# Raw score products of the first pair moved up, in place of products of zeros

## The chip, the cores and the metric

The kernel runs on one core of one Trainium2 chip. The metric is the device time of one execution in microseconds, and lower is better. The time before is the median of three runs.

## The reference

The program is attention, followed by two feed-forward layers. Queries, keys and values come as 2 x 12 heads of 448 positions and 64 elements, all in float32. Cut to what matters here:

```
scores = scale * q @ k.T               # each head: 448 x 448, k=64
scores = where(mask, -1e9, scores)     # causal: later positions masked
scores = scores - max(scores, axis=-1)
attn   = exp(scores); attn = attn / (sum(attn) + 1e-9)
x      = attn @ v                      # 896 tokens x 768
h      = x @ w_in                      # 768 -> 1024, then h * softmax(h), layer norm, g_ln
y      = ln @ w_out                    # 1024 -> 768
out    = max(y @ w_in2, 0)**2 @ w_out2 # 768 -> 2048 -> 768
```

## The kernel before

**Pairs.** Attention works on twelve pairs of heads (pair 0 to pair 11), two heads side by side in the upper and lower 64 partitions. A pair goes through these steps, each with a short name and the pair's number behind a point:

- `load_r`: SP issues the transfer of keys and queries into a buffer `KQ` (four of them).
- `H`: ScalarE copies them, rounded for faster products, to `HI` (three of them).
- `S0c`, `S0a`, `S0b`: TensorE multiplies the rounded copies into a PSUM tile `mxp`, only to find each row's maximum (L253). Each of the three takes a PSUM bank.
- `mxc`, `mxa`, `mxb`: VectorE adds the mask and reduces each product to its maxima `mx` (L268); a reduction is one instruction, and a second one reads its accumulator. Then the bank is given back.
- `mT`, `row`, `rowd`: TensorE transposes the maxima (L280), ScalarE copies them, and SP sends them through DMA into a row `MR` (L297, L298). For pair 0 alone this is replaced by `mxr`: ScalarE copies the maxima to `mr` (L292) and they are subtracted by products with a negative identity (L330).
- `Sa`, `Sb`: the scores of the first and the second half, transposed, into a PSUM tile `s`: first the raw products of keys and queries in full float32 (L311, four products per half, shown as eight records), then the products that subtract the maxima (L330 for pair 0: ten per half; L322 for the others).
- `ea1`, `eb1`: ScalarE takes the exponential of a half into `PP` and gives the bank back (L346).
- `ka`, `kb`, `ad`: GpSimd zeroes the masked half and adds rows. `Ua`, `Ub`, `Us`: TensorE multiplies by the values and sums. Then follow the division, transfers and further steps.

**Order.** The order of all steps on all engines is written out by hand, in one list of names `SEQ`. Each engine takes its own steps out of it, in the list's order, and waits by semaphore for what the other engines must have done. The transfers all go through SP's queue, in the list's order as well.

**Banks.** During attention there are four double banks of PSUM. `bank2` takes the first of a list of free ones when the program is built, and `give` puts a bank back at the list's end. The order of takes and gives in `SEQ` thus sets which bank a step uses and which earlier step it waits for.

**Products of zeros.** `fill(n)` takes a bank, issues `n` products of a tile of zeros (L528) and gives the bank back. The step `fl` calls `fill(2)` whatever its number, and `f1` calls `fill(1)`. Their results are never read.

The start of `SEQ` before:

```
fl.0 load_r.0 H.0 fl.1 fl.2 fl.3 fl.4 f1.0 S0c.0 S0a.0 S0b.0 fl.5 fl.6 fl.7 mxc.0 load_r.1 mxa.0 fl.8 mxb.0 lq.0 H.1 mxr.0
S0b.1 S0a.1 load_r.2 Sa.0 mxb.1 S0c.1 mxa.1 H.2 load_r.3 mxc.1 S0a.2 ea1.0 S0b.2 mT.1 Sb.0 row.1 H.3 ld.3 load_v.0
```

After attention come the two feed-forward layers, whose products (L499 `h`, L656 `y`, L913 `ab`, L1124 `o`) take up the rest of the time. Weights of the first are loaded during attention (`lq`, `ld`).

Of the kernel before, what the change touches and what calls it, by code (L numbers as in the profile page):

```python
# [25 lines left out]
ATT = ("recips", "rcd", "spread", "norm", "x_hi", "x_lo", "E", "Ua", "Ub", "sums")  # L26

SEQ = """
fl.0 load_r.0 H.0 fl.1 fl.2 fl.3 fl.4 f1.0 S0c.0 S0a.0 S0b.0 fl.5 fl.6 fl.7 mxc.0 load_r.1 mxa.0 fl.8 mxb.0 lq.0 H.1 mxr.0
S0b.1 S0a.1 load_r.2 Sa.0 mxb.1 S0c.1 mxa.1 H.2 load_r.3 mxc.1 S0a.2 ea1.0 S0b.2 mT.1 Sb.0 row.1 H.3 ld.3 load_v.0  # L30
mxb.2 lq.1 rowd.1 mxa.2 S0c.2 ka.0 S0b.3 Sa.1 load_r.4 load_v.1 eb1.0 kb.0 mxc.2 ad.0 mT.2 mxb.3 ea1.1 ka.1 lq.2 Sb.1
row.2 S0a.3 S0c.3 Ua.0 load_v.2 rowd.2 H.4 Ub.0 load_r.5 mxa.3 eb1.1 mxc.3 lq.3 S0c.4 kb.1 S0a.4 ad.1 mT.3 Us.0 row.3
Sa.2 mxa.4 E.0 S0b.4 sums.0 ea1.2 Sb.2 mxc.4 mxb.4 recips.0 eb1.2 Ua.1 H.5 Ub.1 load_v.3 lq.8 mT.4 rowd.3 wf.0 Us.1
S0b.5 rcd.0 row.4 Sa.3 load_r.6 E.1 ea1.3 H.6 S0a.5 lq.4 ka.2 mxb.5 Sb.3 mxa.5 eb1.3 S0c.5 rowd.4 Sa.4 ea1.4 mxc.5
Sb.4 kb.2 ad.2 mT.5 S0a.6 ka.3 S0b.6 sums.1 kb.3 spread.0 recips.1 row.5 mxa.6 eb1.4 norm.0 Ua.2 load_r.7 x_hi.0 rcd.1
Ub.2 Us.2 ka.4 S0c.6 H.7 load_v.4 lq.5 mxb.6 rowd.5 E.2 spread.1 mxc.6 Ua.3 S0a.7 x_lo.0 mT.6 sums.2 Ub.3 ad.3 row.6
lq.6 load_r.8 mxa.7 kb.4 S0c.7 rowd.6 S0b.7 recips.2 Us.3 Sb.5 rcd.2 lq.7 norm.1 wh.0 mxc.7 E.3 mxb.7 sums.3 x_hi.1
Ua.4 eb1.5 ad.4 H.8 Sa.5 lq.9 ea1.5 mT.7 x_lo.1 row.7 Sb.6 spread.2 S0b.8 eb1.6 kb.5 Sa.6 S0a.8 recips.3 ea1.6
load_r.9 Ub.4 wf.1 mxb.8 Us.4 S0c.8 mxa.8 H.9 norm.2 E.4 rowd.7 ka.5 mxc.8 rcd.3 Sa.7 S0a.9 load_v.5 Sb.7 ea1.7 mT.8
ad.5 S0b.9 mxa.9 S0c.9 load_r.10 x_hi.2 row.8 Ua.5 kb.6 spread.3 x_lo.2 mxb.9 ka.6 norm.3 Ub.5 sums.4 load_v.6 ad.6  # L40
load_g.0 rowd.8 Us.5 ka.7 wh.1 mxc.9 recips.4 wl.1 Sa.8 H.10 eb1.7 S0a.10 E.5 mT.9 kb.7 load_v.7 Sb.8 ea1.8 S0b.10
rcd.4 load_r.11 row.9 S0c.10 sums.5 mxa.10 mxb.10 Ua.6 Ub.6 mxc.10 spread.4 eb1.8 x_hi.3 Us.6 H.11 x_lo.3 kb.8 lq.10
rowd.9 load_v.8 recips.5 mT.10 norm.4 S0b.11 row.10 rcd.5 mxb.11 E.6 ad.7 ka.8 S0a.11 mxa.11 Ua.7 Ub.7 Sa.9 ad.8
S0c.11 rowd.10 mxc.11 Sb.9 ld.4 mT.11 ea1.9 Sa.10 row.11 eb1.9 wl.0 x_hi.4 Sb.10 sums.6 x_lo.4 rowd.11 Us.7 lq.11
load_v.9 ea1.10 spread.5 Ua.8 eb1.10 Ub.8 kb.9 norm.5 Sb.11 Sa.11 recips.6 Us.8 wf.2 eb1.11 lw.0 wf.3 ea1.11 wh.2 E.7
h1.0 x_hi.5 ld.5 wl.2 wh.3 h1.1 wl.3 rcd.6 ka.9 spread.6 ka.10 x_lo.5 wf.4 kb.11 norm.6 h0.0 ka.11 wh.4 h0.1 h2.0 h1.2
kb.10 sums.7 recips.7 wf.5 rcd.7 E.8 load_v.10 h2.1 sums.8 h2.2 lw.1 h1.3 wl.4 ad.9 h0.2 h2.3 Ua.9 wh.5 x_hi.6 Ub.9
h0.3 wl.5 x_lo.6 recips.8 h0.4 spread.7 h0.5 h1.4 lw.2 h1.5 mx.0 mx.1 ex.0 Us.9 norm.7 E.9 rcd.8 mu.0 h2.4 h2.5 Ua.10
ex.1 sq.0 load_v.11 sums.9 Ub.10 Ua.11 x_hi.7 Ub.11 ad.10 de.0 mu.1 va.0 ad.11 spread.8 recips.9 de.1 Us.10 x_lo.7
sq.1 norm.8 va.1 E.10 mx.2 of.0 rcd.9 sums.10 ex.2 x_hi.8 recips.10 Us.11 x_lo.8 spread.9 pw.0 fa.0 h4.0 h5.0 mu.2  # L50
norm.9 rcd.10 h4.1 h5.1 E.11 pw.1 h5.2 of.1 h4.2 h3.0 sums.11 spread.10 recips.11 ln.0 x_hi.9 x_lo.9 fa.1 h3.1 sq.2
rcd.11 de.2 T.0 h3.3 oh.0 norm.10 x_hi.10 va.2 h3.2 h5.3 ol.0 ln.1 x_lo.10 pw.2 spread.11 Th.0 lw.3 oh.1 of.2 Tl.0
norm.11 ol.1 h3.4 x_hi.11 h4.4 T.1 x_lo.11 of.3 h3.5 mx.3 fa.2 oh.2 h5.4 Th.1 Tl.1 h4.3 h4.5 oh.3 ex.3 ln.2 mu.3 de.3
mx.4 h5.5 sq.3 ex.4 mx.5 va.3 T.2 lw.4 h6.0 ex.5 pw.3 h6.2 lw.5 mu.4 h6.4 de.4 h6.3 de.5 fa.3 lw.6 sq.4 ln.3 T.3 Th.2
mu.5 h6.1 lw.7 Th.3 ol.2 sq.5 Tl.2 Tl.3 va.4 pw.4 h6.5 va.5 mx.6 ol.3 ex.6 fa.4 y0.0 mu.6 of.4 sq.6 of.5 pw.5 oh.4
y0.1 de.6 ol.4 fa.5 of.6 y0.2 oh.5 ln.4 va.6 ln.5 ol.5 oh.6 y0.3 pw.6 y0.4 ol.6 T.4 y0.5 fa.6 Th.4 Tl.4 of.7 ln.6 T.5
y0.6 Th.5 Tl.5 T.6 oh.7 Th.6 ol.7 r2.0 r2.1 y0.7 Tl.6 y1.0 yo.0 yo.1 yo.2 qr.0 r2.2 qh.0 qg.0 qr.1 r2.3 qh.2 qg.2 qr.5
r2.5 s1.1 qr.4 r2.4 s2.1 s4.1 y1.1 yp.0 xt.0 xt.1 yd.0 y1.2 yp.1 xt.2 xl.0 yd.1
"""


def attention_moe_kernel(tc, kq, v, w_in, w_out, g_ln, w_in2, w_out2, out):
# [7 lines left out]
    NP, P, _, S = kq.shape  # L70
    D = P // 2
    DM, NT = out.shape
    H = DM // D
# [19 lines left out]
    with es:  # L93
# [71 lines left out]
        def bank2(nm):  # L165

            pl = slots.pop(0)
            t = pl.tile([P, 2, 512], F32, tag="b", name=nm)
            slot_of[id(t)] = (pl, t)
            return t  # L170
# [9 lines left out]
        with att:  # L180
# [52 lines left out]
            mx = {}  # L233
            mr = {}
            UB = {}
            sb = {}
# [40 lines left out]
            def max_T(i):  # L277

                b = st.pop(("c", i))
                nc.tensor.transpose(b[0:8, 0, 512 - JP :], mx.pop(i), ident[:JP, :JP])  # L280
                return b

            def max_row(i, T):
                st["m2", i] = m2 = work.tile([8, JP], F32R, tag="m2", name="m2")
                nc.scalar.copy(m2, T[0:8, 0, 512 - JP :])
                give(T)
# [14 lines left out]

            HALF = (((0, 64, 0, 448), (3, 0, 384, 64)), ((1, 192, 128, 320), (2, 0, 256, 192)))

            def scores(n):
                i, a = divmod(n, 2)
                K, Q = (KQ[i % NKQ][:, j] for j in range(2))
                s = sb[n] = bank2("s")
                for t, o, q0, nq in HALF[a]:
                    for h in range(2):
                        r = slice(D * h, D * h + D)  # L310
                        nc.tensor.matmul(  # L311
                            s[:, h, o : o + nq],
                            K[r, P * t : P * t + P],
                            Q[r, q0 : q0 + nq],
                            start=t == HALF[a][0][0],
                            stop=False,
                        )

                for o, x, n in () if i in mr else (((0, 0, D + S),), ((192, D + P, S - P), (0, D + 2 * P, S - 2 * P)))[a]:
                    for h in range(2):  # L320
                        r = slice(D * h, D * h + D)
                        nc.tensor.matmul(  # L322
                            s[:, h, o : o + n], NEG1[r], MR[i % 3][r, x : x + n], start=False, stop=o == 0
                        )
                for t, o, q0, nq in HALF[a] if i in mr else ():
                    for h in range(2):
                        for j in range(q0 // JP, 4):
                            c = max(q0 - JP * j, 0)
                            x = o + JP * j + c - q0
                            nc.tensor.matmul(  # L330
                                s[:, h, x : x + JP - c],
                                mr[i][:, 4 * h + j : 4 * h + j + 1].broadcast_to((JP, P)),
                                NID[:, c:JP],
                                start=False,
                                stop=j == 3 and t == HALF[a][-1][0],
                            )

            def causal(n):

                p = PP[n % NPP]  # L340
                for o, m in ((0, D), (D, P)) if n % 2 == 0 else ((0, P), (192, P)):
# [726 lines left out]
            for n in range(1, NQ):  # L1068
# [129 lines left out]
```

## Time and profile before

| | us |
|---|---|
| median of three runs | 431.63 |
| the three runs | 430.87, 431.90, 431.63 |
| the profiled execution's own time | 431.36 |
| its span in the profile | 429.6 |

The span reaches from the first instruction to the last that the profiler shows; the execution's own time holds what lies around it as well. In rows of the trace, PE is TensorE's products and PEld its weight loads, DVE is VectorE, ACT ScalarE, POOL GpSimd and SP the engine that issues the transfers. An arrow `<-` in a pair of brackets names what ended an engine's idle time.

### The profile page before, as it was taken

The numbers are of one execution on the slowest core, as the hardware profiler recorded it, in microseconds if no ns is written. First come the engines' busy times: TensorE is split into PE (matmuls) and PEld (weight loads), VectorE is DVE, ScalarE is ACT, GpSimd is POOL, SyncE is SP. The second block draws the span as 40 slices with busy tenths as digits, with TensorE's granted clock in tenths as the row PEclk, the third lists the DMA queues.
The fourth block names the chain that finished last, engine by engine and source line by source line (L and its number), as shares of the span: only waits on it lengthen the run. The fifth ranks groups of instructions, "written<-read, shape, count | busy, mean of one in ns | idle before, by whom it ended". The sixth has DMA issues, their size and how long they took to land.

```text
span 429.6 us, 6467 instructions
## 1 busy us (share of the span) xinstructions
PE 423.4 (99%) x2425; PEld 361.3 (84%) x2425; DVE 319.4 (74%) x582; ACT 199.2 (46%) x282; POOL 151.9 (35%) x145
## 2 busy tenths in 40 slices
PE   8999999999999999999999999999999999999996
PEld 6666656876888999888999999999899988999995
DVE  6897885997889886597897999999767767434221
ACT  3567765435658545234745445465463242111101
POOL 1499797799320010300023321233303133131310
PEclk9999999999999999999999999999999999999999
DMA  7566666451160700440013443335123425542403
GB/s 248 202 206 198 195 156 228 155 189 52 44 243 0 279 16 0 148 146 2 1 54 94 146 148 115 105 82 158 58 73 84 137 76 167 181 148 74 146 2 128
DMA packets 33001, 52.46 MB, mean 122 GB/s; under 512 B 5962, under 2 KB 24394, under 8 KB 32586
## 3 DMA queue, kind: packets, MB, share of 16 engines
q1 hardware_dynamic: 32970, 52.05, 38.5%
q8 instruction: 19, 0.31, 0.3%
q14 instruction: 12, 0.10, 0.1%
HBM read 49.16 MB, written 2.80 MB: 121 GB/s over the span
## 4 chain that ended last, share of the span: by engine, by line
PE 61%; issue 25%; POOL 6%; DVE 5%; DMA 1%; ACT 1%; POOLq 0%; DVEq 0%
PE o L1124 15%; PE h L499 14%; PE y L656 13%; PE s L311 5%; PE U L355 5%; POOL q L822 3%; POOL w L970 3%; PE mxp L253 2%; PE fill L528 2%; DVE T L742 2%; PE T L634 1%; PE U L379 1%; PE s L322 1%; DMA KQ<-in_kq_dram 1%; DVE F L742 1%
## 5 line engine op out<-in xcount | busy, mean ns | idle before, releaser
L1124 PE MATMUL o<-gh,w 128*128 128x480 f32 (+1 forms) x552 | 113.2, 364 | 0.1
L1124 PEld LDWEIGHTS o<-gh,w 128*128 128x128 f32 x552 | 102.9, 188 | 8.9 <-POOL w L970 1.4
L913 PE MATMUL ab<-yT,q 128*128 128x448 f32 x306 | 65.1, 366 | 0.0
L913 PEld LDWEIGHTS ab<-yT,q 128*128 128x128 f32 x306 | 57.6, 188 | 4.5
L970 POOL TENSOR_TENSOR w<-wf,w 128x768 fp32r<-128x768 f32 x16 | 29.9, 1873 | 87.1 <-ACT w L969 87.1
L499 PE MATMUL h<-w,xT 128*128 128x512 f32 x252 | 59.5, 394 | 0.0
L656 PE MATMUL y<-lnT,w 128*128 128x384 f32 (+1 forms) x288 | 58.7, 363 | 0.0
L656 PEld LDWEIGHTS y<-lnT,w 128*128 128x128 f32 x288 | 52.0, 188 | 5.6
L499 PEld LDWEIGHTS h<-w,xT 128*128 128x128 f32 x252 | 46.7, 188 | 10.2 <-issue 0.6
L268 DVE CUSTOM_DVE_ANT_0 JK<-mxp,MK 112x336 bf16<-112x336 f32 (+2 forms) x96 | 38.8, 446 | 10.9 <-PE mxp L253 10.0
L969 ACT CAST w<-wf 128x768 fp32r<-128x768 f32 x16 | 13.4, 835 | 69.0 <-DVE wf L153 58.8
L913 PE MATMUL ab<-T,q 128*128 128x448 f32 x175 | 38.9, 366 | 0.0
L151 DVE TENSOR_SCALAR wf<-raw 128x768 int32<-128x768 int32 (+1 forms) x30 | 18.5, 618 | 26.3 <-DMA raw<-in_moe_w_out_dram 21.2
L913 PEld LDWEIGHTS ab<-T,q 128*128 128x128 f32 x175 | 32.9, 188 | 2.5
L822 POOL TENSOR_TENSOR q<-wk,q 128x768 fp32r<-128x768 f32 x9 | 17.1, 1898 | 50.7 <-ACT q L818 50.7
L343 POOL TENSOR_SCALAR_AFFINE_SELECT PP<-PP 128x256 f32<-128x256 f32 (+1 forms) x48 | 29.0, 635 | 14.4 <-ACT PP L346 14.4
L153 DVE SCALAR_TENSOR_TENSOR wf<-raw,wf 128x768 int32<-128x768 int32 (+1 forms) x30 | 32.9, 1098 | 1.0
L822 POOL TENSOR_TENSOR q<-ws,q 128x768 fp32r<-128x768 f32 x7 | 13.4, 1908 | 56.8 <-ACT q L818 56.8
L152 DVE SCALAR_TENSOR_TENSOR wf<-raw,wf 128x768 int32<-128x768 int32 (+1 forms) x30 | 31.4, 1047 | 1.0
L346 ACT ACTIVATE PP<-s 128x1024 f32<-128x1024 f32 x24 | 24.4, 1023 | 12.1 <-PE s L322 7.7
L742 DVE TENSOR_TENSOR gh<-gf,gh 128x896 fp32r<-128x896 f32 x15 | 20.2, 1391 | 12.4 <-ACT gh L745 12.4
L311 PE MATMUL s<-KQ 64*128 64x448 f32 (+3 forms) x192 | 26.9, 399 | 0.0
(117 smaller groups left out, 601.4 us busy)
## 6 DMA issues: line engine op xcount, KB each, us to landing
raw<-in_moe_w_out_dram SPq DMA_DIRECT2D x24, 768.0 KB
raw<-in_moe_w_in_dram SPq DMA_DIRECT2D x16, 768.0 KB
KQ<-in_kq_dram SPq DMA_DIRECT2D x12, 448.0 KB
raw<-in_moe_w_in_dram SPq DMA_DIRECT2D x12, 256.0 KB
raw<-in_moe_w_in_dram SPq DMA_DIRECT2D x3, 1024.0 KB
VR<-in_v_dram SPq DMA_DIRECT2D x12, 256.0 KB
bc<-d SPq DMA_DIRECT2D x24, 112.0 KB
out_dram<-o SPq DMA_DIRECT2D x6, 240.0 KB
```

What stands on the lines that cost most here:

```text
L152: nc.vector.scalar_tensor_tensor(xi, hw, -0x40000000, xi, ALU.bitwise_and, ALU.bitwise_or)
L153: nc.vector.scalar_tensor_tensor(xi, lw, 29, xi, ALU.logical_shift_right, ALU.bitwise_or)
L268: nc.vector.tensor_tensor_reduce(JK[t], b[0:JP, h, o : o + nk], MK[:, S - nk :], 1.0, NEG, ALU.add, ALU.max, mx[i][:, 4 * h + t : 4 * h + ...
L311: nc.tensor.matmul(s[:, h, o : o + nq], K[r, P * t : P * t + P], Q[r, q0 : q0 + nq], start=t == HALF[a][0][0], stop=False,)
L343: nc.gpsimd.affine_select(ap, ap, [[0, 2], [1, m]], ALU.is_ge, 0.0, base=0, channel_multiplier=-1)
L499: nc.tensor.matmul(b[:, half, :], xT[c][s][:, t * P : t * P + P], W1[c][:, w, 512 * half : 512 * half + 512], start=(c == 0 and s == 0 and ...
L656: nc.tensor.matmul(b[:, ci, 0:n], WO[fi][:, w, c * P : c * P + P], M["lnT"][a][s][:, fi, :], start=(fi == 0 and w == 0 and s == 0), stop=( ...
L742: nc.vector.tensor_tensor(o_, a, b, ALU.subtract)
L822: (eng or nc.vector).tensor_tensor(lo, q_src(n, g), f(hi), ALU.subtract)
L913: nc.tensor.matmul(b, w[r // 2][:, o + P * c : o + P * c + P], xs[c][r % 2], start=first and q == 0, stop=last and q == len(ps) - 1,)
L970: nc.gpsimd.tensor_tensor(W2[m][:, 1], x, f(W2[m][:, 0]), ALU.subtract)
L1124: nc.tensor.matmul(flat(b)[:, o : o + n], w[:, wp, c : c + P], ops[s][:, x : x + n], start=first and r == 0, stop=last and r == 2,)
```

## The change

Four steps `fl.5` to `fl.8` go, each with two products of zeros. In their place, right behind the products for pair 0's maxima, stands a new step `Pa.0`: the raw products of pair 0's first half, which were the first part of `Sa.0`. `Sa.0` keeps its place and issues the rest, the ten products that subtract the maxima. `S0b.1` stands ahead of `mxr.0` now and not behind it. The other steps of the list keep their order.

```diff
-fl.0 load_r.0 H.0 fl.1 fl.2 fl.3 fl.4 f1.0 S0c.0 S0a.0 S0b.0 fl.5 fl.6 fl.7 mxc.0 load_r.1 mxa.0 fl.8 mxb.0 lq.0 H.1 mxr.0
-S0b.1 S0a.1 load_r.2 Sa.0 mxb.1 S0c.1 mxa.1 H.2 load_r.3 mxc.1 S0a.2 ea1.0 S0b.2 mT.1 Sb.0 row.1 H.3 ld.3 load_v.0
+fl.0 load_r.0 H.0 fl.1 fl.2 fl.3 fl.4 f1.0 S0c.0 S0a.0 S0b.0 Pa.0 mxc.0 load_r.1 mxa.0 mxb.0 lq.0 H.1 S0b.1 mxr.0 S0a.1
+load_r.2 Sa.0 mxb.1 S0c.1 mxa.1 H.2 load_r.3 mxc.1 S0a.2 ea1.0 S0b.2 mT.1 Sb.0 row.1 H.3 ld.3 load_v.0 mxb.2 lq.1
...
-            def scores(n):
+            def raw_scores(n):
                 i, a = divmod(n, 2)
                 K, Q = (KQ[i % NKQ][:, j] for j in range(2))
                 s = sb[n] = bank2("s")
...
+            def scores(n):
+                i, a = divmod(n, 2)
+                if n not in sb:
+                    raw_scores(n)
+                s = sb[n]
                 for o, x, n in () if i in mr else (((0, 0, D + S),), ((192, D + P, S - P), (0, D + 2 * P, S - 2 * P)))[a]:
...
                 OPS["S" + x] = lambda i, a=a: scores(2 * i + a)
+                OPS["P" + x] = lambda i, a=a: raw_scores(2 * i + a)
```

## Rows read from the trace of the kernel before

**Rows 1.** The page: busy time, share of the span and instructions of each engine.

```profile
PE 423.4 (99%) x2425; PEld 361.3 (84%) x2425; DVE 319.4 (74%) x582; ACT 199.2 (46%) x282; POOL 151.9 (35%) x145
```

**Rows 2.** The chain of waits, 0 to 60 us: start us, us, what.

```profile
1.10 4.48 PE fill L528 x11
5.58 1.26 PE mxp L253 x6
6.84 0.80 PE fill L528 x2
...
9.74 0.67 PE mxp L253 x5
10.41 0.92 PE s L311 x8
11.33 1.23 PE s L330 x10
12.56 0.32 PE mxp L253 x2
...
12.90 0.39 DVE JK L268
...
13.79 0.26 PE mxp L280
14.05 1.06 PE s L311 x8
...
55.96 0.48 PE s L311
56.44 5.05 DMA KQ<-in_kq_dram
```

**Rows 3.** Timeline, 6 to 15 us: start us, us, engine, line, operation [idle before <-releaser].

```profile
6.50 0.94 ACT L243 CAST HI<-KQ 128x896 fp32r<-128x896 f32 x1 [1.04 <-DMA KQ<-in_kq_dram]
...
8.19 0.08 DVE L268 DVE_READ_ACCUMULATOR2_ANT mx<- 112x1 f32 x1
...
9.09 0.30 PEld L528 LDWEIGHTS fill<-Z 128*128 128x128 f32 x2 [0.41 <-PE fill L528]
...
9.44 0.08 DVE L268 DVE_READ_ACCUMULATOR2_ANT mx<- 112x1 f32 x1
9.56 0.20 ACT L292 CAST mr<-mx 112x8 fp32r<-112x8 f32 x1 [2.12 <-DVE mx L268]
...
10.19 0.51 DVE L268 CUSTOM_DVE_ANT_0 JK<-mxp,MK 112x336 bf16<-112x336 f32 x1 [0.66 <-PE mxp L253]
...
10.38 0.94 ACT L243 CAST HI<-KQ 128x896 fp32r<-128x896 f32 x1 [0.62 <-DMA KQ<-in_kq_dram]
...
11.44 0.08 DVE L268 DVE_READ_ACCUMULATOR2_ANT mx<- 112x1 f32 x1
11.44 0.62 DVE L268 CUSTOM_DVE_ANT_0 JK<-mxp,MK 112x448 bf16<-112x448 f32 x1
...
12.60 1.02 ACT L346 ACTIVATE PP<-s 128x1024 f32<-128x1024 f32 x1 [1.28 <-PE s L330]
12.65 0.08 DVE L268 DVE_READ_ACCUMULATOR2_ANT mx<- 112x1 f32 x1
12.90 0.39 DVE L268 CUSTOM_DVE_ANT_0 JK<-mxp,MK 112x224 bf16<-112x224 f32 x1 [0.17 <-PE mxp L253]
...
14.36 0.67 SPq L297 DMA_DIRECT2D MR<-m  x1
```

**Rows 4.** Two stretches: us, busy us of each engine, clock, DMA share, GB/s.

```profile
13.00:14.00 1.00, 0.56 (x9) 0.28 (x7) 0.96 (x5) 0.62 (x1) 0.31 (x2) 1.00 0.29 111
200.00:430.00 230.00, 225.38 (x1111) 207.60 (x1109) 157.35 (x189) 89.29 (x116) 56.03 (x30) 1.00 0.33 102
```

**Rows 5.** Weight loads of the products of zeros, first eleven, then eight: ns min/median/max.

```profile
L528 PEld LDWEIGHTS fill<-Z x11: 289/337/338, 1.1 to 4.6; 128*128 128x128 f32 x11
...
L528 PEld LDWEIGHTS fill<-Z x8: 186/190/334, 6.8 to 9.2; 128*128 128x128 f32 x8
```

More of the change, by code (lines that the diff above doesn't have):

```diff
@@ L28 @@
 SEQ = """
-fl.0 load_r.0 H.0 fl.1 fl.2 fl.3 fl.4 f1.0 S0c.0 S0a.0 S0b.0 fl.5 fl.6 fl.7 mxc.0 load_r.1 mxa.0 fl.8 mxb.0 lq.0 H.1 mxr.0
-S0b.1 S0a.1 load_r.2 Sa.0 mxb.1 S0c.1 mxa.1 H.2 load_r.3 mxc.1 S0a.2 ea1.0 S0b.2 mT.1 Sb.0 row.1 H.3 ld.3 load_v.0
-mxb.2 lq.1 rowd.1 mxa.2 S0c.2 ka.0 S0b.3 Sa.1 load_r.4 load_v.1 eb1.0 kb.0 mxc.2 ad.0 mT.2 mxb.3 ea1.1 ka.1 lq.2 Sb.1
-row.2 S0a.3 S0c.3 Ua.0 load_v.2 rowd.2 H.4 Ub.0 load_r.5 mxa.3 eb1.1 mxc.3 lq.3 S0c.4 kb.1 S0a.4 ad.1 mT.3 Us.0 row.3
-Sa.2 mxa.4 E.0 S0b.4 sums.0 ea1.2 Sb.2 mxc.4 mxb.4 recips.0 eb1.2 Ua.1 H.5 Ub.1 load_v.3 lq.8 mT.4 rowd.3 wf.0 Us.1
@@ L34 @@
[L34 to L58, printed above, removed]
+fl.0 load_r.0 H.0 fl.1 fl.2 fl.3 fl.4 f1.0 S0c.0 S0a.0 S0b.0 Pa.0 mxc.0 load_r.1 mxa.0 mxb.0 lq.0 H.1 S0b.1 mxr.0 S0a.1
@@ new lines @@
+load_r.2 Sa.0 mxb.1 S0c.1 mxa.1 H.2 load_r.3 mxc.1 S0a.2 ea1.0 S0b.2 mT.1 Sb.0 row.1 H.3 ld.3 load_v.0 mxb.2 lq.1
+rowd.1 mxa.2 S0c.2 ka.0 S0b.3 Sa.1 load_r.4 load_v.1 eb1.0 kb.0 mxc.2 ad.0 mT.2 mxb.3 ea1.1 ka.1 lq.2 Sb.1 row.2 S0a.3
+S0c.3 Ua.0 load_v.2 rowd.2 H.4 Ub.0 load_r.5 mxa.3 eb1.1 mxc.3 lq.3 S0c.4 kb.1 S0a.4 ad.1 mT.3 Us.0 row.3 Sa.2 mxa.4
+E.0 S0b.4 sums.0 ea1.2 Sb.2 mxc.4 mxb.4 recips.0 eb1.2 Ua.1 H.5 Ub.1 load_v.3 lq.8 mT.4 rowd.3 wf.0 Us.1 S0b.5 rcd.0
+row.4 Sa.3 load_r.6 E.1 ea1.3 H.6 S0a.5 lq.4 ka.2 mxb.5 Sb.3 mxa.5 eb1.3 S0c.5 rowd.4 Sa.4 ea1.4 mxc.5 Sb.4 kb.2 ad.2
@@ new lines @@
+mT.5 S0a.6 ka.3 S0b.6 sums.1 kb.3 spread.0 recips.1 row.5 mxa.6 eb1.4 norm.0 Ua.2 load_r.7 x_hi.0 rcd.1 Ub.2 Us.2 ka.4
+S0c.6 H.7 load_v.4 lq.5 mxb.6 rowd.5 E.2 spread.1 mxc.6 Ua.3 S0a.7 x_lo.0 mT.6 sums.2 Ub.3 ad.3 row.6 lq.6 load_r.8
+mxa.7 kb.4 S0c.7 rowd.6 S0b.7 recips.2 Us.3 Sb.5 rcd.2 lq.7 norm.1 wh.0 mxc.7 E.3 mxb.7 sums.3 x_hi.1 Ua.4 eb1.5 ad.4
+H.8 Sa.5 lq.9 ea1.5 mT.7 x_lo.1 row.7 Sb.6 spread.2 S0b.8 eb1.6 kb.5 Sa.6 S0a.8 recips.3 ea1.6 load_r.9 Ub.4 wf.1
+mxb.8 Us.4 S0c.8 mxa.8 H.9 norm.2 E.4 rowd.7 ka.5 mxc.8 rcd.3 Sa.7 S0a.9 load_v.5 Sb.7 ea1.7 mT.8 ad.5 S0b.9 mxa.9
@@ new lines @@
+S0c.9 load_r.10 x_hi.2 row.8 Ua.5 kb.6 spread.3 x_lo.2 mxb.9 ka.6 norm.3 Ub.5 sums.4 load_v.6 ad.6 load_g.0 rowd.8
+Us.5 ka.7 wh.1 mxc.9 recips.4 wl.1 Sa.8 H.10 eb1.7 S0a.10 E.5 mT.9 kb.7 load_v.7 Sb.8 ea1.8 S0b.10 rcd.4 load_r.11
+row.9 S0c.10 sums.5 mxa.10 mxb.10 Ua.6 Ub.6 mxc.10 spread.4 eb1.8 x_hi.3 Us.6 H.11 x_lo.3 kb.8 lq.10 rowd.9 load_v.8
+recips.5 mT.10 norm.4 S0b.11 row.10 rcd.5 mxb.11 E.6 ad.7 ka.8 S0a.11 mxa.11 Ua.7 Ub.7 Sa.9 ad.8 S0c.11 rowd.10 mxc.11
+Sb.9 ld.4 mT.11 ea1.9 Sa.10 row.11 eb1.9 wl.0 x_hi.4 Sb.10 sums.6 x_lo.4 rowd.11 Us.7 lq.11 load_v.9 ea1.10 spread.5
@@ new lines @@
+Ua.8 eb1.10 Ub.8 kb.9 norm.5 Sb.11 Sa.11 recips.6 Us.8 wf.2 eb1.11 lw.0 wf.3 ea1.11 wh.2 E.7 h1.0 x_hi.5 ld.5 wl.2
+wh.3 h1.1 wl.3 rcd.6 ka.9 spread.6 ka.10 x_lo.5 wf.4 kb.11 norm.6 h0.0 ka.11 wh.4 h0.1 h2.0 h1.2 kb.10 sums.7 recips.7
+wf.5 rcd.7 E.8 load_v.10 h2.1 sums.8 h2.2 lw.1 h1.3 wl.4 ad.9 h0.2 h2.3 Ua.9 wh.5 x_hi.6 Ub.9 h0.3 wl.5 x_lo.6
+recips.8 h0.4 spread.7 h0.5 h1.4 lw.2 h1.5 mx.0 mx.1 ex.0 Us.9 norm.7 E.9 rcd.8 mu.0 h2.4 h2.5 Ua.10 ex.1 sq.0
+load_v.11 sums.9 Ub.10 Ua.11 x_hi.7 Ub.11 ad.10 de.0 mu.1 va.0 ad.11 spread.8 recips.9 de.1 Us.10 x_lo.7 sq.1 norm.8
@@ new lines @@
+va.1 E.10 mx.2 of.0 rcd.9 sums.10 ex.2 x_hi.8 recips.10 Us.11 x_lo.8 spread.9 pw.0 fa.0 h4.0 h5.0 mu.2 norm.9 rcd.10
+h4.1 h5.1 E.11 pw.1 h5.2 of.1 h4.2 h3.0 sums.11 spread.10 recips.11 ln.0 x_hi.9 x_lo.9 fa.1 h3.1 sq.2 rcd.11 de.2 T.0
+h3.3 oh.0 norm.10 x_hi.10 va.2 h3.2 h5.3 ol.0 ln.1 x_lo.10 pw.2 spread.11 Th.0 lw.3 oh.1 of.2 Tl.0 norm.11 ol.1 h3.4
+x_hi.11 h4.4 T.1 x_lo.11 of.3 h3.5 mx.3 fa.2 oh.2 h5.4 Th.1 Tl.1 h4.3 h4.5 oh.3 ex.3 ln.2 mu.3 de.3 mx.4 h5.5 sq.3
+ex.4 mx.5 va.3 T.2 lw.4 h6.0 ex.5 pw.3 h6.2 lw.5 mu.4 h6.4 de.4 h6.3 de.5 fa.3 lw.6 sq.4 ln.3 T.3 Th.2 mu.5 h6.1 lw.7
@@ L59 @@
+Th.3 ol.2 sq.5 Tl.2 Tl.3 va.4 pw.4 h6.5 va.5 mx.6 ol.3 ex.6 fa.4 y0.0 mu.6 of.4 sq.6 of.5 pw.5 oh.4 y0.1 de.6 ol.4
+fa.5 of.6 y0.2 oh.5 ln.4 va.6 ln.5 ol.5 oh.6 y0.3 pw.6 y0.4 ol.6 T.4 y0.5 fa.6 Th.4 Tl.4 of.7 ln.6 T.5 y0.6 Th.5 Tl.5
+T.6 oh.7 Th.6 ol.7 r2.0 r2.1 y0.7 Tl.6 y1.0 yo.0 yo.1 yo.2 qr.0 r2.2 qh.0 qg.0 qr.1 r2.3 qh.2 qg.2 qr.5 r2.5 s1.1 qr.4
+r2.4 s2.1 s4.1 y1.1 yp.0 xt.0 xt.1 yd.0 y1.2 yp.1 xt.2 xl.0 yd.1
 """
```

## The prediction

> **What bounds the kernel now.** I read the page first: TensorE (PE) is busy 423.4 us of a span of 429.6 us [rows 1], so it idles 6.2 us in all, and 4.6 us of those lie behind 200 us [rows 4], nearly all at the very end, when the last results are copied out. Next comes the chain of waits, the work that ended last, followed back. From 14.05 us to 56.44 us it is TensorE work without a gap, 68 pieces of which the group gives the first and the last [rows 2]; then one transfer of keys (5.05 us), which is issued in the moment when TensorE has finished with the buffer that it overwrites; then TensorE again [rows 2]. So what happens in the first 14 us is passed on: TensorE's place in its program at 14 us sets all that follows.
>
> Ahead of 14 us the chain runs through TensorE too, but 2.90 us of it (6.84 to 9.74 us) are products of zeros, four calls of two each, which do nothing for the result [rows 2]. The reader should not take 2.90 us for the gain. The timeline says what the real work waits for. VectorE's reductions for pair 0 end with the reading of an accumulator at 9.44 us, and ScalarE's copy `mr` of the maxima follows at 9.56 us and takes 0.20 us [rows 3]. The ten products with `mr` (L330) can't start before that, whatever TensorE does. VectorE then stands idle 0.66 us for the first products of pair 1, and 0.17 us again for their last group at 12.90 us [rows 3]. When it has reduced that group, TensorE's transposition of pair 1's maxima follows at 13.79 us, and the scores of the second half at 14.05 us [rows 2]. So the end of this stage is set by VectorE, and 0.83 us of VectorE's time in it is waiting.
>
> **The change, part by part.**
>
> *Removed:* `fl.5` to `fl.8`, eight products of zeros and their weight loads (four calls of two). Nothing reads their bank. What they take from the path is 9.74 - 6.84 = 2.90 us [rows 2].
>
> *Moved:* the raw products of pair 0's first half (L311, eight records) stand at 10.41 us and take 0.92 us [rows 2]; they go to 6.84 us. They need only the keys and queries, which have landed when pair 0's products for maxima, made from a copy of them, begin at 5.58 us [rows 2], and a bank. The bank is the one that the removed products used: banks are handed out in order of return, and with the four calls gone every later request gets the same bank as before. So no new wait for a bank arises; the scores hold it through 6.84 to 9.74 us, where the zeros held it. No DMA moves with this step and no queue is passed. That `S0b.1` now stands ahead of `mxr.0` changes nothing, since one is TensorE's and the other ScalarE's.
>
> *What the moved products cost there.* The weight loads of the first eleven products of zeros took 337 ns (median), those of the later eight 190 ns, with the first of these still at 334 ns [rows 5]: TensorE ran at the lower of its two levels, 1.2 GHz, at the start and reached 2.4 GHz shortly after 6.84 us. So the 0.92 us are the lower bound and twice that, 1.84 us, the upper. Behind them come pair 1's products `S0b.1` and `S0a.1`, 0.67 us [rows 2]. Their operand is ready when ScalarE's copy ends at 6.50 + 0.94 = 7.44 us, and the bank of the second group is free at 8.19 + 0.08 = 8.27 us [rows 3]. So these products end between about 8.7 us (8.27 us, a signal of some 0.1 us, half of 0.67 us) and 6.84 + 1.84 + 0.67 = 9.35 us. I take 8.7, because the later of the eight weight loads are fast. Either end is ahead of 9.44 us, when VectorE gets to them, so the uncertainty costs nothing.
>
> *TensorE.* It then has nothing until `mr` is there, at 9.56 + 0.20 = 9.76 us; with some 0.1 us for the signal (VectorE's last reading, 9.44 + 0.08 us, and ScalarE's start at 9.56 us lie 0.04 us apart) the ten products begin at about 9.9 us in place of 11.33 us, 1.4 us earlier, and end at 12.56 - 1.4 = 11.16 us [rows 2, 3]. The 1.2 us from 8.7 to 9.9 us are the cover that is gone: TensorE idles in them, and nothing real is late by it.
>
> *ScalarE.* The exponential of the first half began at 12.60 us, 1.28 us after the engine was free [rows 3]. It would now begin at about 11.33 us: the copy for pair 2 ahead of it on the queue waits for a transfer and runs from 10.38 to 11.32 us [rows 3], and the transfer doesn't move. It hands its bank on at 12.35 us, ahead of the second half's scores.
>
> *VectorE, which sets the end.* The first reduction of pair 1 starts with the last accumulator's reading at 9.44 us (at 11.44 us a reading and the next reduction start together, [rows 3]) in place of 10.19 us: 0.75 us. The wait at 12.90 us goes too, since `S0c.1` now comes behind products that end at 11.16 us: 12.90 - 12.65 = 0.25 us [rows 3]. Sum 1.00 us. If a gap stays as large as the reading itself at both places, it is 0.66 + 0.17 = 0.83 us, the lower bound; the upper one is the 1.4 us of the ten products, were VectorE not in between. I take 1.00: the row at 11.44 us is the same change of group. So the transposition comes at 12.79 us and the second half at 13.05 us.
>
> *What follows.* The row of maxima goes to memory at 14.36 us, and the later loads are queued behind it on SP [rows 3]; all of them come 1.0 us earlier with it. The loads issued at the start are nearly done by then: the DMA share falls to 0.29 in 13 to 14 us [rows 4]. From there every engine keeps its place to the others, and the 1.00 us is carried to the end.
>
> The sum: 431.36 us, the profiled execution's own time (span 429.6 and 1.76 around it), less 1.00 is 430.36 us. That execution lies 0.27 us under the median of the runs, 431.63 us; against the median it is 430.6 us, which I give. It is 0.23% less, and under the 0.3% (1.3 us) that a measurement of this kernel can tell from no change.
>
> **The rivals.**
>
> *All of TensorE's 1.4 us arrive.* VectorE would have to shorten elsewhere, or the earlier exponential help the stage behind (GpSimd starts on its result). For it: ScalarE's 1.28 us of waiting [rows 3]. Against it: the transposition waits for VectorE [rows 2]. Time 430.2 us, counted as faster. Chance 0.17.
>
> *Nothing arrives.* The 1.0 us is taken back between 14 and 76 us, by a wait that now shows. The place would be the key transfer at 56.44 us: if it were held by traffic rather than by its issue, it would land at the same time as before. Against it: it is issued when TensorE frees the buffer [rows 2], so it moves along. Time 431.6 us. Chance 0.13.
>
> *The clock falls, and it is slower.* The zeros kept TensorE at work from 6.84 to 9.74 us, if only with 0.41 us of waiting in a pair [rows 3]. Without them it idles 1.2 us ahead of 9.9 us, and again between 11.16 and 12.79 us but for a few products. If the clock fell to 1.2 GHz there, TensorE would lose 1 - 190/337 = 0.44 us in each us of the fall [rows 5]. Ahead of 12.79 us it has that to spare; behind it every loss counts. A fall of 2.3 us behind 12.79 us eats the gain of 1.0 us: from there on the change is slower. The low stretch at the start lasted from 1.10 us to past 6.84 us, some 5.7 us [rows 2, 5]; a fall as long costs 5.7 x 0.44 = 2.5 us, 1.5 us more than is won: 433.1 us. For it: rows 5, the clock isn't always full. Against it: in 13 to 14 us TensorE is busy for 0.56 us and the granted clock is 1.00 [rows 4]. Chance 0.08.
>
> The Trainium skill, page "TensorE: Matmul & The Clock Gate", section "Why this matters for your kernels", says that the clock is kept by TensorE's activity and that gaps between bursts of products bring it back to half. That speaks against this change, which opens gaps; by it the time would be that of the rival above. No row of this trace shows a fall inside the kernel.
>
> **How the numbers follow.** The forecast, 0.8 to 1.2 us gained, has 0.62, the rivals 0.17, 0.13 and 0.08. Run to run the shown times differ by 1.03 us, so a median moves by some 0.3 us. Faster by over 0.3%: most of the first rival and a fourth of the forecast, 0.31. Slower by over 0.3%: most of the clock's case, 0.07. Same: 0.62. The range holds the forecast and, up to 2 in 10 left out, its neighbours: from 430.2 less 0.4, 429.8, to the second rival's 431.6.
>
> **What would show it.** Right: eight L311 records right behind pair 0's products near 6.8 us; the ten products with `mr` (L330) near 9.9 us; no wait of VectorE at its change to pair 1 and a reduction there at 9.44 us; the transposition (L280) near 12.8 us; the last key transfer issued near 55.4 us; a span near 428.6 us. Wrong: weight loads over 300 ns behind 9 us (the clock); a transposition earlier than 12.6 us (first rival); a 12.8 us transposition with the key transfer still at 56.4 us, or a new wait between them (second rival).

## The result and the profile after

The changed kernel takes 433.77 us (median of four runs, 433.66 to 434.43) beside 431.49 us for the kernel before (four runs): ratio 1.0061, 95% interval 1.0044 to 1.0077. It is 2.3 us slower, where 1.0 us faster was forecast. One thing is needed to read the numbers below: the moment at which TensorE's clock rises and falls isn't the same in each execution, so the undisturbed runs of one kernel can lie in two groups, and then both are given; five disturbed runs of the experiments, at 436.22, 697.33, 841.01, 842.95 and 843.13 us, are left out of their medians and ratios. A ratio with its interval needn't be the quotient of the two medians.

The page of the changed kernel: its span, the busy times, and of the rows in 40 slices the granted clock in tenths.

```profile
span 432.0 us, 6453 instructions
...
PE 424.3 (98%) x2417; PEld 361.6 (84%) x2417; DVE 320.2 (74%) x582; ACT 199.0 (46%) x282; POOL 153.2 (35%) x145
...
PEclk9599999999999999999999999999999999999999
```

One digit of the last row is new, a 5 in the second slice (10.8 to 21.6 us). The kernel before has 9 throughout, and TensorE busy nearly all the time in 8 to 10 us; its row, and its stretch (us; busy us of PE, PEld, DVE, ACT, POOL; granted clock; DMA share; GB/s):

```profile
PEclk9999999999999999999999999999999999999999
```
```profile
8.00:10.00 2.00, 1.89 (x12) 0.93 (x10) 1.52 (x10) 0.20 (x1) 0.00 (x0) 1.00 1.05 414
```

The same view of the changed kernel:

```profile
7.00:8.00 1.00, 0.55 (x10) 0.37 (x6) 0.96 (x3) 0.02 (x1) 0.00 (x0) 1.00 0.88 323
8.00:9.00 1.00, 0.47 (x2) 0.21 (x2) 1.00 (x7) 0.00 (x0) 0.00 (x0) 1.00 1.08 416
9.00:10.00 1.00, 0.28 (x3) 0.31 (x3) 1.00 (x9) 0.50 (x2) 0.00 (x0) 1.00 1.13 457
10.00:11.00 1.00, 1.00 (x12) 0.96 (x10) 1.00 (x6) 0.64 (x1) 0.00 (x0) 0.97 1.03 432
11.00:12.00 1.00, 0.89 (x6) 0.47 (x6) 0.97 (x5) 0.97 (x1) 0.00 (x0) 0.50 0.93 381
13.00:14.00 1.00, 1.00 (x5) 0.78 (x6) 1.00 (x7) 0.96 (x2) 0.00 (x0) 0.50 0.34 127
...
18.00:20.00 2.00, 2.00 (x14) 1.18 (x10) 1.90 (x12) 0.39 (x1) 1.46 (x3) 0.50 1.03 372
20.00:22.00 2.00, 2.00 (x15) 1.21 (x15) 0.00 (x0) 1.28 (x3) 1.85 (x2) 0.70 0.17 60
22.00:24.00 2.00, 2.00 (x22) 1.17 (x22) 1.32 (x5) 1.62 (x2) 1.38 (x4) 1.00 0.01 2
```

The clock is 1.00 up to 10 us, though TensorE is busy only 0.47 and 0.28 us of the two us from 8 on. It falls just ahead of 11 us, to 0.50, which is 1.2 GHz, and stays there until past 20 us, through a stretch in which TensorE is busy nearly all the time (0.89 us of 11 to 12 us, and every us shown behind that in full). Then it is back. What that does is in the timeline of the same kernel (start us, us, engine, line, operation, idle before and its releaser):

```profile
6.13 1.14 PE L311 MATMUL s<-KQ 64*128 64x448 f32 x8
...
8.25 0.47 PE L253 MATMUL mxp<-HI 64*128 64x448 f32 x2 [0.70 <-DVE mx L268]
...
9.26 0.08 DVE L268 DVE_READ_ACCUMULATOR2_ANT mx<- 112x1 f32 x1
9.29 0.51 DVE L268 CUSTOM_DVE_ANT_0 JK<-mxp,MK 112x336 bf16<-112x336 f32 x1
...
9.72 1.27 PE L335 MATMUL s<-NID,mr 112*128 112x112 f32 x10 [1.01 <-ACT mr L292]
...
11.03 1.02 ACT L351 ACTIVATE PP<-s 128x1024 f32<-128x1024 f32 x1 [0.39 <-PE s L335]
...
12.65 0.35 PE L280 MATMUL mxp<-ident,mx 112*8 112x112 f32 x1
...
14.94 2.21 PEld L335 LDWEIGHTS s<-NID,mr 112*128 112x128 f32 x10 [0.44 <-issue]
...
17.85 0.39 DVE L268 CUSTOM_DVE_ANT_0 JK<-mxp,MK 112x224 bf16<-112x224 f32 x1 [2.44 <-PE mxp L253]
```

Down to 12.65 us this is the forecast, nearly row by row. The raw products stand at 6.13 us; the ten products with `mr` begin at 9.72 us (9.9 foretold); VectorE passes from pair 0 to pair 1 with 0.03 us between the reading at 9.26 us and the reduction at 9.29 us, where it had waited 0.66 us [rows 3]; the exponential starts at 11.03 us (11.33 foretold); the transposition comes at 12.65 us, 1.14 us ahead of 13.79 us [rows 2]. Behind it the weight loads of the second half's ten products take 2.21 us, where the chain of before gave 1.23 us to such a ten in all [rows 2], and VectorE waits 2.44 us for products. The kernel before has that wait too, but shorter, 0.52 us:

```profile
16.71 0.39 DVE L268 CUSTOM_DVE_ANT_0 JK<-mxp,MK 112x224 bf16<-112x224 f32 x1 [0.52 <-PE mxp L253]
```

The chain of waits shows what became of the lead:

```profile
12.72 0.28 PE mxp L280
13.00 2.01 PE s L311 x8
15.01 2.31 PE s L335 x10
17.32 0.88 PE mxp L253 x5
```

The second half's raw products take 2.01 us (1.06 before, [rows 2]) and the ten behind them 2.31 us (1.23 for the first half's, [rows 2]). The last transfer of keys, which TensorE releases, was issued at 56.44 us before [rows 2]; SP's timeline of the changed kernel has it here:

```profile
59.10 0.61 SPq L209 DMA_DIRECT2D KQ<-in_kq_dram  x1
```

That is 2.66 us later, and the span ends 432.0 - 429.6 = 2.4 us later. The loss is complete by the key transfer; nothing behind adds to it.

### The profile page after: what moved, and what is told of

Its sections match the earlier page's. It is cut to its first block, busy times and chain, and to the rows that moved or that the text cites. A ratio compares the mean times of both kernels' runs of the same rounds, so it can differ in the third digit from the quotient of the medians.

```text
span 432.0 us, 6453 instructions
## 1 busy us (share of the span) xinstructions
PE 424.3 (98%) x2417; PEld 361.6 (84%) x2417; DVE 320.2 (74%) x582; ACT 199.0 (46%) x282; POOL 153.2 (35%) x145
## 4 chain that ended last, share of the span: by engine, by line
PE 61%; issue 25%; POOL 6%; DVE 4%; ACT 2%; DMA 1%; POOLq 0%; DVEq 0%
PE o L1130 15%; PE h L505 13%; PE y L662 13%; PE s L311 6%; PE U L360 5%; POOL q L828 3%; POOL w L976 3%; PE mxp L253 2%; PE T L640 1%; PE s L327 1%; PE U L384 1%; DMA KQ<-in_kq_dram 1%; PE s L335 1%; ACT q L824 1%; DVE F L748 1%
## 5 line engine op out<-in xcount | busy, mean ns | idle before, releaser
L828 POOL TENSOR_TENSOR q<-wk,q 128x768 fp32r<-128x768 f32 x9 | 18.2, 2018 | 50.7 <-ACT q L824 50.7
L153 DVE SCALAR_TENSOR_TENSOR wf<-raw,wf 128x768 int32<-128x768 int32 (+1 forms) x30 | 32.9, 1096 | 1.0
L152 DVE SCALAR_TENSOR_TENSOR wf<-raw,wf 128x768 int32<-128x768 int32 (+1 forms) x30 | 32.3, 1075 | 1.0
L311 PE MATMUL s<-KQ 64*128 64x448 f32 (+3 forms) x192 | 29.1, 425 | 0.0
```

What stands on the lines that cost most here:

```text
L152: nc.vector.scalar_tensor_tensor(xi, hw, -0x40000000, xi, ALU.bitwise_and, ALU.bitwise_or)
L153: nc.vector.scalar_tensor_tensor(xi, lw, 29, xi, ALU.logical_shift_right, ALU.bitwise_or)
L311: nc.tensor.matmul(s[:, h, o : o + nq], K[r, P * t : P * t + P], Q[r, q0 : q0 + nq], start=t == HALF[a][0][0], stop=False,)
L828: (eng or nc.vector).tensor_tensor(lo, q_src(n, g), f(hi), ALU.subtract)
```

## The experiments

**Theory 1:** the zeros were what kept the clock up; without them TensorE idles, and the chip grants 1.2 GHz for some 10 us. **Theory 2:** the clock goes along, but the raw products' new place costs: the scores hold a bank from 6 us on and everything behind comes in another order. Three tools were used: products of zeros put back, zeros left out with nothing moved, and further real work put into the gap. Where a step `zp` stands in an experiment, zeros are added into the bank that the first half's scores hold already (they add nothing to the sums and need no other bank):

```diff
+            def zeros_in(n):
+                for j in range(n):
+                    nc.tensor.matmul(
+                        sb[0][:, j % 2, 0:S], Z, Z[:, 0:1].broadcast_to((P, S)), start=False, stop=False
+                    )
+            OPS["zp"] = zeros_in
```

**Zeros in the gap ahead of the ten products.**

```diff
-... Pa.0 mxc.0 load_r.1 mxa.0 mxb.0 lq.0 H.1 S0b.1 mxr.0 S0a.1 load_r.2 ...
+... Pa.0 mxc.0 load_r.1 mxa.0 mxb.0 lq.0 H.1 S0b.1 mxr.0 S0a.1 zp.5 load_r.2 ...
```

> The changed kernel with five products of zeros added into the first half's own bank, right behind pair 1's products and ahead of the ten products with mr; they add nothing to the scores and need no bank of their own. They fill some 1 us of the idle time and nothing else is changed. Theory 1: the clock stays up, 430.6 us. Theory 2: 433 to 434 us.

430.44 us beside 430.95 us of the kernel before, ratio 0.9997 (0.9973 to 1.0021). Nine of eleven runs lie at 429.85 to 430.80 us with a mean granted clock of 0.998 to 1.0, two at 433.98 us with 0.992. With five products more, the changed kernel loses its loss in nine of eleven runs. The kernel before isn't free of the fall either: one of its 29 runs beside these took 434.20 us, with 0.994. The two windows that matter, and the transposition, from its trace:

```profile
8.00:10.00 2.00, 2.00 (x14) 1.52 (x13) 2.00 (x15) 0.20 (x1) 0.00 (x0) 1.00 1.09 419
10.00:12.00 2.00, 1.78 (x15) 1.30 (x14) 1.97 (x9) 1.60 (x2) 0.00 (x0) 1.00 0.98 405
```
```profile
8.61 1.22 PE L540 MATMUL s<-Z 128*128 128x448 f32 x5
9.68 1.27 PE L335 MATMUL s<-NID,mr 112*128 112x112 f32 x10
...
12.60 0.26 PE L280 MATMUL mxp<-ident,mx 112*8 112x112 f32 x1 [0.18 <-DVE mx L268]
```

Here TensorE is busy for 2.00 us in 8 to 10 us, the clock stays at 1.00, and the transposition lies at 12.60 us. Theory 2 foretold 433 to 434 us; it is ruled out, since the raw products, the bank and the order are those of the changed kernel.

**Two zeros in place of five.**

```diff
-... S0b.1 mxr.0 S0a.1 load_r.2 ...
+... S0b.1 mxr.0 S0a.1 zp.2 load_r.2 ...
```

> As the run with five products of zeros in the gap, but with two, some 0.4 us. Theory 1: a smaller dose; if 0.4 us less idling is enough, 430.6 us; if not, 433 to 434 us; some runs either way would give a spread between. Theory 2: 433 to 434 us in every run.

434.77 us, 1.0100 (1.0086 to 1.0115), with a mean granted clock of 0.986 to 0.987 in each of the four runs. Two products aren't enough.

**The same dose at another place,** in the earlier gap alone:

```diff
-... S0b.0 Pa.0 mxc.0 load_r.1 ...
+... S0b.0 Pa.0 zp.5 mxc.0 load_r.1 ...
```

> The changed kernel with five products of zeros right behind the moved raw products alone, the gap ahead of the ten products with mr left open. Theory 1: the dose of the run with zeros in the gap at another place; if idling as such counts, the clock falls in few runs and the median is near 430.6 us; if the place counts, it falls in more, and the median is 433 to 435 us, as with the two calls of zeros. Theory 2: 433 to 434 us in every run.

434.28 us, 1.0048 (1.0020 to 1.0076): four runs at 429.87 to 431.50 us with a clock of 0.994 to 1.0, eight at 433.82 to 435.50 us with 0.987 to 0.992. It is the second of Theory 1's two answers: at this place the same five products help in fewer runs than in the later gap.

In another run two calls of the old `fl`, four products, stand there:

```diff
-... S0b.0 Pa.0 mxc.0 load_r.1 ...
+... S0b.0 Pa.0 mxc.0 fl.5 fl.6 load_r.1 ...
```

> The raw products stay at their new place, and two calls of two products of zeros each come back behind them, ahead of pair 1's products for maxima. Theory 1 (the clock: without the zeros TensorE idles and its clock falls to 1.2 GHz for some 10 us): the clock stays at 2.4 GHz, the transposition stays near 12.7 us as in the changed kernel, and the forecast gain appears: 430.6 us, 1.0 us under before. Theory 2 (the place of the raw products is what costs: the scores hold their bank from 6 us on and all that follows comes in another order): still 433 to 434 us, whatever the zeros do.

434.07 us, 1.0057 (1.0028 to 1.0086): three runs at 429.76 to 430.67 us with a clock of 0.998 or 0.999, seven at 433.92 to 435.69 us with 0.986 to 0.990. The expected 430.6 us came in three runs of ten only: with the raw products moved, covering the earlier gap isn't enough, and the time goes with the clock in each group. The profiled execution of this kernel is one of the quick ones: the clock is 1.00 in it up to 30 us, the transposition is at 12.65 us, and it takes 429.76 us with a span of 428.0 us, more than the forecast gain.

**Zeros at both places.**

```diff
-... Pa.0 mxc.0 load_r.1 mxa.0 mxb.0 lq.0 H.1 S0b.1 mxr.0 S0a.1 load_r.2 ...
+... Pa.0 zp.5 mxc.0 load_r.1 mxa.0 mxb.0 lq.0 H.1 S0b.1 mxr.0 S0a.1 zp.5 load_r.2 ...
```

> The changed kernel with five products of zeros right behind the moved raw products and five more behind pair 1's products for maxima, all added into the first half's own bank. TensorE has then next to no idle time from 5.5 to 11 us. Theory 1 (the clock falls after idling): the clock stays up in every run, more surely than with either group alone, and the time is 430.0 to 430.4 us, 0.6 to 1.0 us under before. Theory 2 (the raw products' place): no better than the run with zeros in the gap; 430.6 us or more.

430.67 us beside 431.23 us, 0.9988 (0.9975 to 1.0000). All eleven runs lie at 430.24 to 431.61 us with a clock of 0.998 to 1.0. The clock did what Theory 1 foretold, the time did not (430.0 to 430.4 us), and Theory 2's 430.6 us or more would allow it; what decides between the two is the run above with zeros in the later gap alone. It is the best version found: half a microsecond under before, at the edge of what can be told from no change. Its only trace is of the execution at 843.13 us, so how the clock went in the eleven is known from their means alone.

**No zeros, nothing moved:** the kernel before without `fl.5` to `fl.8`.

```diff
-... S0b.0 fl.5 fl.6 fl.7 mxc.0 load_r.1 mxa.0 fl.8 mxb.0 ...
+... S0b.0 mxc.0 load_r.1 mxa.0 mxb.0 ...
```

> The kernel before without the steps fl.5 to fl.8, nothing moved: the raw products stand behind pair 1's products and end right ahead of the ten products with mr. Theory 1: the idle time is smaller at 8.7 to 9.9 us and larger ahead of it; if what counts is the work in the whole stretch, the clock falls as in the changed kernel and the time is 433 to 434 us; if the last 1.2 us of idling counted, it stays up and the time is 430.6 us. Theory 2: no raw product is moved ahead, so it isn't slower than before: 430.5 to 431.5 us.

432.62 us, 1.0053 (1.0023 to 1.0083). Five runs lie at 430.37 to 430.82 us (clock 0.994 to 1.0), two at 432.50 and 432.73 us (0.996), five at 434.42 to 436.01 us (0.983 to 0.988). The profiled one fell early:

```profile
6.00:8.00 2.00, 0.56 (x10) 0.39 (x8) 1.92 (x9) 0.94 (x1) 0.00 (x0) 1.00 0.87 284
8.00:10.00 2.00, 2.00 (x14) 1.13 (x10) 2.00 (x15) 0.63 (x2) 0.00 (x0) 0.61 1.09 438
10.00:12.00 2.00, 2.00 (x11) 1.93 (x10) 1.76 (x8) 0.50 (x1) 0.00 (x0) 0.50 0.98 403
```

The removal of the zeros alone brings the fall in five of twelve runs for certain (two more lie between the groups), with the raw products where they always stood. Both answers that I had foreseen occur, one in some runs and one in others.

**More real work in the gap:** both halves' raw products are moved up, and pair 1's groups take the next banks.

```diff
-... Pa.0 mxc.0 load_r.1 mxa.0 mxb.0 lq.0 H.1 S0b.1 mxr.0 S0a.1 load_r.2 ...
+... Pa.0 mxc.0 Pb.0 load_r.1 mxa.0 lq.0 H.1 S0b.1 mxb.0 mxr.0 S0a.1 load_r.2 ...
```

> The second half's raw products too are moved up, behind the first half's, into the bank that is free first; pair 1's first products take the next bank, and no zeros are added. Real work covers 7.1 to 8.2 us of the idle time, and the stage behind the transposition has 1.06 us less to do on TensorE. Theory 1: where the clock stays up 429.0 to 429.6 us; since 0.6 us of idling and more remain from 8.6 to 9.7 us, it may still fall in some runs, and these lie some 3.5 to 5 us higher. Theory 2: scores that hold two banks early cost more than one: 434 us or more in all runs.

432.52 us, 1.0036 (1.0018 to 1.0054); the clock is 0.987 to 0.992 in all twelve runs. Its trace:

```profile
8.00:9.00 1.00, 0.72 (x8) 0.33 (x4) 1.00 (x7) 0.00 (x0) 0.00 (x0) 1.00 1.01 374
9.00:10.00 1.00, 0.46 (x3) 0.28 (x3) 1.00 (x9) 0.20 (x1) 0.00 (x0) 1.00 1.15 465
...
11.00:12.00 1.00, 0.54 (x5) 0.31 (x4) 0.96 (x5) 1.00 (x2) 0.00 (x0) 0.89 0.96 395
12.00:14.00 2.00, 1.97 (x11) 1.69 (x12) 1.25 (x9) 0.89 (x3) 0.67 (x2) 0.50 0.66 251
...
16.00:20.00 4.00, 4.00 (x27) 2.54 (x25) 2.04 (x12) 1.73 (x4) 3.18 (x4) 0.67 0.76 248
```

The work was moved out of the stage behind and into the gap. Some of the gap is left (0.72 and 0.46 us busy in 8 to 10 us), TensorE now lacks the moved work at 11 to 12 us, and the clock falls there; which of the two idle stretches brought it down, this trace doesn't show. With zeros behind pair 1's first group:

```diff
-... H.1 S0b.1 mxb.0 mxr.0 S0a.1 load_r.2 ...
+... H.1 S0b.1 zp.3 mxb.0 mxr.0 S0a.1 load_r.2 ...
```

> As the run with both halves' raw products moved up, with three products of zeros behind pair 1's first group, where TensorE waits for a bank. Theory 1: the clock stays up in more of the runs than without them, and the median is 429.0 to 429.6 us, under both kernels. Theory 2: 434 us or more.

433.18 us, 1.0049 (1.0029 to 1.0068), clock 0.988 to 0.994 in all nine runs. In its trace the clock falls later:

```profile
10.00:11.00 1.00, 1.00 (x9) 0.79 (x9) 1.00 (x7) 0.62 (x1) 0.00 (x0) 1.00 1.09 459
11.00:12.00 1.00, 0.88 (x8) 0.65 (x7) 0.96 (x5) 0.70 (x2) 0.00 (x0) 1.00 0.91 368
12.00:13.00 1.00, 0.78 (x6) 0.51 (x6) 0.73 (x6) 0.64 (x1) 0.29 (x2) 1.00 0.92 350
13.00:14.00 1.00, 1.00 (x13) 0.90 (x10) 0.68 (x5) 0.60 (x2) 0.38 (x2) 1.00 0.24 90
14.00:16.00 2.00, 1.67 (x12) 1.32 (x11) 1.97 (x11) 1.51 (x2) 0.17 (x1) 0.50 0.05 16
```

The expectation was wrong: TensorE is busy all the time from 8 to 11 us here, and the clock falls all the same, behind the idle time from 11 us on. So zeros were put there too, `zq` being the same step on the second half's bank:

```diff
-... S0b.1 zp.3 mxb.0 mxr.0 S0a.1 load_r.2 Sa.0 mxb.1 S0c.1 mxa.1 ... ea1.0 S0b.2 mT.1 ...
+... S0b.1 zp.4 mxb.0 mxr.0 S0a.1 load_r.2 Sa.0 mxb.1 S0c.1 zq.4 mxa.1 ... ea1.0 S0b.2 zq.2 mT.1 ...
```

> Both halves' raw products moved up as in the earlier run with both, and zeros wherever TensorE idled in its trace: four behind pair 1's first group, four behind pair 1's last group and two ahead of the transposition, all added into the banks of the scores. If the low clock alone kept that version from its gain, the clock stays up now, the transposition stays near 12.7 us and the time is 429.0 to 429.6 us, under both kernels. If TensorE then idles behind 14 us for VectorE, the clock may still fall there, and the time is 431 us or more.

431.15 us beside 431.10 us, 1.0009 (0.9988 to 1.0030); ten of eleven runs at 430.43 to 432.52 us with a clock of 0.997 to 1.0, one at 435.02 us with 0.996. The clock stays up, but the zeros now delay real work:

```profile
11.50 1.03 PE L540 MATMUL s<-Z 128*128 128x448 f32 x4
...
12.46 0.68 PE L253 MATMUL mxp<-HI 64*128 64x448 f32 x6
...
13.29 0.51 DVE L268 CUSTOM_DVE_ANT_0 JK<-mxp,MK 112x336 bf16<-112x336 f32 x1 [0.75 <-PE mxp L253]
...
13.56 0.26 PE L280 MATMUL mxp<-ident,mx 112*8 112x112 f32 x1
```

VectorE waits 0.75 us for pair 2's products, which stand behind zeros, and the transposition is at 13.56 us. Not all of that is the zeros' doing: with both raw products moved and no zeros it is at 13.13 us already, beside 12.65 us in the changed kernel. My 429.0 to 429.6 us weren't reached.

**The kernel before once more,** for a second trace.

> The kernel before, unchanged, for a second trace of it: where the clock rises earlier than at 7 us, pair 0's reductions should begin some 0.2 us sooner and the transposition should lie near 13.6 us in place of 13.79 us. That would account for part of the gain that the run with zeros in the gap doesn't show against before's median (0.5 us where 1.0 was forecast).

431.10 us, one execution, span 429.4 us:

```profile
6.09 0.30 PEld L528 LDWEIGHTS fill<-Z 128*128 128x128 f32 x2
...
8.79 0.45 PEld L253 LDWEIGHTS mxp<-HI 64*128 64x128 f32 x6 [0.28 <-ACT HI L243]
...
12.91 0.26 PE L280 MATMUL mxp<-ident,mx 112*8 112x112 f32 x1 [0.44 <-DVE mx L268]
```

At 6.09 us two weight loads of zeros take 0.30 us together: here the clock had risen already, where the first load of these eight still took 334 ns in the trace that I read [rows 5]. So the same eight zeros were done sooner; pair 1's products waited for ScalarE's copy at 8.79 us and no longer for zeros until 9.67 us, and the transposition is at 12.91 us, not at 13.79 us. That is 0.88 us sooner, where I had expected some 0.2 us.

But this lead doesn't arrive: the span is 429.4 us beside 429.6 us. The chains of waits show where it goes, first that of the trace read before the prediction, then this one:

```profile
44.94 0.19 PE mxp L280
...
52.81 0.19 PE mxp L280
```
```profile
44.30 0.19 PE mxp L280
...
45.84 4.03 DMA KQ<-in_kq_dram
...
53.02 0.19 PE mxp L280
```

At 44 us TensorE is still 0.64 us ahead, at 53 us it is 0.21 us behind, and between them the chain runs through a transfer of keys, which it doesn't in the first trace. SP issued it 0.54 us later than there (45.84, not 45.30 us), in both traces right behind the transfer `bc<-d`, which waits for another transfer.

## Why the prediction was wrong

**What held.** The moved products, their bank, the start of the ten products with `mr`, VectorE as what sets the end of the stage, and the transposition: foretold at 12.79 us, found at 12.65 us. That it lies so far ahead of 13.79 us is in part luck: the clock rose sooner in this execution, and in the second trace of the kernel before the transposition is at 12.91 us with nothing changed. That what TensorE loses or wins around 14 us is passed on holds for the loss: 2.66 us at the last key transfer, 2.4 us at the end of the span. It doesn't hold to a few tenths: the second trace of the kernel before had won 0.88 us at the transposition and 0.2 us at the end.

**The step that failed** is the one in which the zeros' removal was costed: "The 1.2 us from 8.7 to 9.9 us are the cover that is gone: TensorE idles in them, and nothing real is late by it." What was late by it is all work of TensorE from 10.9 to 21 us, done at 1.2 GHz: the second half's raw products took 2.01 us in place of 1.06 us. The runs show it from both sides: the zeros gone with nothing moved, and the clock falls in five to seven of twelve runs; the products moved with zeros in both gaps, and it falls in none of eleven.

**The rival was there, with its price, and got 0.08.** By its own rate, 0.44 us lost in each us of the low level, the 8.5 us from the transposition at 12.65 us to 21.2 us (0.70 in 20 to 22 us is 1.2 us at half and 0.8 us in full) cost 3.7 us, less the 1.1 us won: 2.6 us, beside the 2.66 us measured at the last key transfer. That it agrees to a tenth is in part luck, as the second trace of before shifts by 0.85 us against the first between 44 and 53 us, with nothing changed in the kernel. Where it was mis-sized is the length (5.7 us were taken from the low stretch at the start, some 10 us came) and the chance. What was held against it, 13 to 14 us with TensorE busy 0.56 and a clock of 1.00 [rows 4], was a single short stretch after a full one. In the changed kernel 8 to 10 us hold 0.75 us of work, and 7 to 8 us only 0.55 us. The forecast should have laid out TensorE's idle time by stretches, before and after; instead it priced each gap by what waits behind it.

The rule of the Trainium skill that stood beside that rival (page "TensorE: Matmul & The Clock Gate", section "Why this matters for your kernels": gaps between bursts of products bring the clock back to half) spoke against the change, and the clock did fall, to 0.50 from 11 us on. But the page says it of gaps above a stated length, and no idle piece here reaches that: the longest of the changed kernel is 1.01 us. So by the rule with its condition the clock would have stayed up, and the trace differs from it: the prediction named the rule without the condition, and that its warning came true is in part luck.

**The size of the gain** was off too. Where the clock stays up, the best version gains 0.5 us, not 1.0. The forecast's 0.75 us for VectorE's wait came from one execution, in which the clock rose late: pair 0's products took 1.33 us in place of the second trace's 0.78 us, and the zeros behind them held up pair 1's products. In the second trace the transposition is at 12.91 us; against that the zeros in the gap (12.60 us) win 0.3 us, against the first trace 1.2 us. How many executions of before are of either kind isn't shown: only two were traced. Nor is a lead at the transposition the gain at the end, as the step "the 1.00 us is carried to the end" had it: over the first trace, the run with zeros in the gap leads by 1.19 us there and ends 0.9 us sooner, the quick run with two calls of zeros by 1.14 us and ends 1.6 us sooner. What the 0.5 us is made of stays open.

**The other rivals.** The 1.4 us didn't arrive. That the lead is taken back by a transfer isn't what made the changed kernel slower, but it happens: in the second trace of before, and at another transfer than the one that the prediction watched.

One reading of the prediction was off without effect: of the 4.6 us of idle time behind 200 us, 0.4 us lie behind the end of the span.

## What to carry to other kernels

Work that computes nothing can still pay for itself: before products of zeros are taken out or replaced, count what TensorE has left to do in that stretch, and price a fall of the clock over what follows, not over the gap. Real work moved forward into a gap leaves a gap where it came from. A cost read from one execution's start should be read from a second one as well, when it depends on when the clock rose; and whether a lead at the start arrives is read at the end of the span, in more than one trace.

## What the runs showed of the hardware

No single idle piece of TensorE in the changed kernel is longer than about 1 us (0.70 us at 8.25 us and 1.01 us at 9.72 us, in its timeline), and the clock fell all the same. It then stayed at 0.50 for some 10 us, while the profile counted TensorE busy for 0.89 us or more of every us; with both raw products moved it was back before 20 us. So a busy TensorE in the profile doesn't mean that the clock will rise, and what decides when it comes back stays open.

The profile's clock is to be trusted only from its first change on. It shows 1.00 at the start, where weight loads of 337 ns tell of the lower level [rows 5]. In the execution of 843.13 us it shows 1.00 to the end, while TensorE is busy for 836.1 of 841.4 us and its 128x480 products (`o`) take 644 ns on average, 376 ns in the kernel before: the clock never rose in it. Why isn't known.

The mean granted clock of a run goes with its time in most runs (0.983 to 0.992 with 431.65 us and more), but not in every one: 0.994 stands at 430.69 us and 0.996 at 435.02 us, and one run of the kernel before shows 0.947 at 431.16 us, of which no trace exists. A quick run's 0.998 needn't be a loss: in the second trace of before the clock falls only behind 420 us (0.96 in 420 to 428 us).
